# A second chunk transposed by DMA, the loads behind it rearranged, and the inverse 32-point units moved next to the forward ones

## The chip, the cores and the metric

One core of one Trainium2 chip. Times are device microseconds of one execution; the profile gives the span of that execution, some 1.9 us less. A ratio is the mean time of one kernel's fast runs over that of the kernel before in the same rounds on the same chip, so it is not quite the ratio of the medians. Kernels are compared only within the same rounds.

On one core a run counts as slow when it is over 1.5% above the fastest of the same kernel.

## The reference, cut to what matters

```python
# x: [1, 2048, 512] bf16; w_r, w_i: [2048, 257]; w_gate, w_up: [512, 1792]; w_down: [1792, 512]
xn  = layernorm(x)                              # rows of 512
A   = irfft2(rfft2(xn) * (w_r + 1j * w_i))      # 2048 x 512 transform, filter, inverse
B   = (gelu(xn @ w_gate) * (xn @ w_up)) @ w_down
out = x + A + B
```

## The kernel before: the parts that matter

TensorE does everything heavy. The gated unit (branch B) runs in four chunks of 512 rows, and the transform (branch A) is cut into small units that are slotted between its matmuls: "D" (along a row), "A" (64-point), "B" (32-point forward), "C" (32-point inverse), "E" and "F". Each unit's result is copied out of the matmul memory by ScalarE or VectorE (an eviction). Every step that follows another matmul group is a numbered hook; the plan puts calls at hooks. Each engine executes its own list in order.

The transposed, normalised rows `xnT` feed both branches; on the way to the D units VectorE adds and subtracts halves of them (the butterflies). Chunks 2 and 3 are transposed by DMA, chunk 1 (the second) by TensorE:

```python
if m < 2:
    at(t, (trans, m, (0, 1), (0, 1, 2, 3)))            # 8 TensorE transposes, copy by VectorE
    at(t + 1, (trans, m, (2, 3), (0, 1, 2, 3), "act")) # 8 more, copy by ScalarE
else:
    at(n + 1, (trans_dma, m))                          # one DMA transpose, issued by SyncE
```

A transform unit "A" of one quarter is stored to DRAM and reloaded in another layout; the first B reads all four quarters:

```python
def units_A(m):        # ... matmuls, eviction by ScalarE, then four stores:
    dma("act" if late_one and ri else "sp", scr1[...], tt[i]...)
def load_tv(m):        # two reloads; each waits until the quarter's stores have landed
    dma("sp", tv[...], scr1[...], r=[("scr1", 2 * m + g, ri) for g in range(2) for ri in range(2)], ...)
def unit_B(g):
    op("pe", ..., r=["be"] + TVK, ...)                 # TVK: every quarter's reload
```

The filter comes in eight slices, each of four loads on GpSimd's queue (`w_r`) and four on SyncE's (`w_i`); GpSimd copies its last column (number 256) apart. `load_late` makes a load wait until TensorE has come to the hook:

```python
def load_late(dst, src, keys, also=(), eng="pool"):
    op(eng, lambda e: e.dma_start(dst, src), ..., dma=True, after=[("pe", pr.cnt["pe"])])
# load_W(s): ... "sp" if k else "pool"
```

So SyncE's list carries the transposes, the stores and reloads of the quarters, and half of the filter. A load that stands ahead of a store in this list is issued ahead of it.

## Time and profile before

| | before |
|---|---|
| time, median (range) | 179.55 us (179.51 to 180.07) |
| span of the profiled run | 177.6 us |
| TensorE busy | 172.6 us, 97% |
| TensorE idle | 5.0 us, at the two ends |
| granted clock | 1.00 |

An engine at 97% busy over the whole span is read by its list: every microsecond of it is on the path, and whatever other engines do counts only where TensorE waits for it. The lines are in the prediction. SyncE's timeline (start, length, what): the stores and the reload of the third quarter, and the stores of the last one, whose reload at 64.58 us is in the prediction:

```profile
52.86 3.65 SPq L346 DMA_DIRECT2D scr<-early  x4
58.39 1.17 SPq L346 DMA_DIRECT2D tv<-scr  x2
59.60 1.94 SPq L346 DMA_DIRECT2D scr<-early  x3
```

### The profile page before, as it was taken

Reading aid. Unit: us, or ns where it says so; the run is one execution under the profiler, and the core shown is the slowest. Engines: PE = TensorE matmul, PEld = TensorE weight load, DVE = VectorE, ACT = ScalarE, POOL = GpSimd, SP = SyncE. Lnnn points to the kernel's source line nnn. Section 1 sums busy time; section 2 is a strip of 40 time slices with the busy share of each in tenths; the row PEclk is TensorE's granted clock in tenths of the full one; section 3 lists DMA queues with packets and bytes.
Section 4 is the critical chain, followed back from the end, with each engine's and each line's share of the span. In section 5 each row is a group of like instructions: output and inputs, shape, how many; then the busy total and the mean of one; then the engine's idle time right before and its main releaser. Section 6 shows DMA issues by size and latency. Waiting matters only on the chain.

```text
span 177.6 us, 3792 instructions
## 1 busy us (share of the span) xinstructions
PE 172.6 (97%) x1394; PEld 107.0 (60%) x1394; DVE 132.3 (74%) x329; ACT 93.5 (53%) x156; POOL 54.3 (31%) x107
## 2 busy tenths in 40 slices
PE   7999999999999999999999999999999999999992
PEld 2576564544566666566564655566766666656881
DVE  2768899986478967776785649797877777897552
ACT  3343557763677523546666665336678577632110
POOL 2210534025142056394850000011444635530000
PEclk9999999999999999999999999999999999999999
DMA  4999999799998579679771304591166646551104
GB/s 122 292 271 318 314 278 340 188 177 225 189 182 173 142 209 193 99 219 226 211 202 28 103 15 122 107 318 52 31 117 108 124 97 118 92 90 30 30 6 118
DMA packets 31059, 27.89 MB, mean 157 GB/s; under 512 B 7120, under 2 KB 27984, under 8 KB 30912
## 3 DMA queue, kind: packets, MB, share of 16 engines
q1 hardware_dynamic: 25936, 19.75, 45.4%
q0 software_dynamic: 4272, 7.24, 19.0%
q10 hardware_dynamic: 832, 0.66, 1.4%
q8 instruction: 11, 0.18, 0.5%
q14 instruction: 8, 0.07, 0.1%
HBM read 18.19 MB, written 6.29 MB: 138 GB/s over the span
## 4 chain that ended last, share of the span: by engine, by line
PE 92%; DMA 4%; SPq 2%; DVE 0%; issue 0%
PE ps L906 27%; PE ps L890 27%; PE ps L792 25%; DMA wu<-in_B_w_up_dram 4%; PE ps L620 2%; SPq L346 2%; PE ps L846 2%; PE ps L648 2%; PE ps L595 2%; PE ps L495 1%; PE ps L467 1%; PE ps L466 1%; PE ps L498 1%; PE ps L463 1%; PE ps L464 1%; PE ps L422 1%
## 5 line engine op out<-in xcount | busy, mean ns | idle before, releaser
L890 PE MATMUL ps<-xnT,wg 128*128 128x512 f16 (+2 forms) x244 | 58.0, 362 | 0.2 <-DMA wg<-in_B_w_gate_dram 0.2
L906 PE MATMUL ps<-xnT,wu 128*128 128x512 f16 (+1 forms) x240 | 57.9, 365 | 0.3 <-DMA wu<-in_B_w_up_dram 0.3
L912 DVE TENSOR_TENSOR hT<-ps,gl 128x512 bf16<-128x512 f32 (+1 forms) x60 | 38.9, 652 | 21.7 <-PE ps L906 15.7
L894 ACT ACTIVATE gl<-ps 128x512 bf16<-128x512 f32 (+1 forms) x60 | 34.2, 569 | 38.5 <-PE ps L890 37.3
L906 PEld LDWEIGHTS ps<-xnT,wu 128*128 128x128 bf16 x240 | 22.5, 98 | 20.5 <-issue 0.8
L890 PEld LDWEIGHTS ps<-xnT,wg 128*128 128x128 bf16 x244 | 22.7, 98 | 16.3 <-issue 1.0
L349 POOL DMA_DIRECT2D wring<-in_A_w_r_dram x32 | 18.7, 637 | 14.6 <-PE ps L792 5.4
L657 POOL COPY tv<-tv 1x128 bf16<-1x128 bf16 x16 | 5.4, 338 | 42.0 <-ACT tv L655 41.9
L792 PE MATMUL ps<-wd,hT 128*128 128x256 bf16 x112 | 14.4, 273 | 0.0
L872 POOL DMA_DIRECT2D x_sb<-tv x16 | 13.2, 865 | 3.4 <-DVE tv L865 2.4
L606 DVE TENSOR_TENSOR early<-early,wring 128x1024 bf16<-128x1024 f16 x16 | 10.3, 687 | 3.8 <-ACT early L601 3.8
L811 ACT ACTIVATE ps<-ps 128x256 f32<-128x256 f32 x16 | 5.9, 371 | 12.9 <-PE ps L792 12.8
L393 DVE BATCH_NORM_STATS2 st<-x_sb 128x6 f32<-128x512 bf16 x16 | 10.6, 682 | 2.2 <-DMA x_sb<-in_A_x_dram 2.2
L792 PEld LDWEIGHTS ps<-wd,hT 128*128 128x128 bf16 x112 | 10.7, 98 | 2.5
L401 POOL TENSOR_TENSOR rstd<-vpe,mhalf 128x4 f32<-128x4 f32 (+2 forms) x6 | 5.0, 836 | 23.1 <-DVE vpe L400 23.1
L471 ACT ACTIVATE early<-ps 128x512 f16<-128x512 f32 x16 | 9.5, 597 | 4.2 <-PE ps L467 4.2
L792 PE MATMUL ps<-arena,xnT 128*128 128x256 f16 x91 | 11.4, 273 | 0.0
L852 ACT ACTIVATE tv<-ps 128x512 bf16<-128x512 f32 x16 | 9.5, 595 | 3.6 <-PE ps L846 3.6
L655 ACT ACTIVATE tv<-ps 128x512 bf16<-128x512 f32 x16 | 9.5, 595 | 3.2 <-PE ps L648 3.2
L601 ACT ACTIVATE early<-ps 128x1024 f16<-128x1024 f32 x8 | 8.2, 1023 | 4.8 <-PE ps L595 4.8
L792 PEld LDWEIGHTS ps<-arena,xnT 128*128 128x128 f16 x91 | 8.5, 98 | 2.3 <-DVE tw L815 0.2
L675 DVE TENSOR_TENSOR x_sb<-ps,tw 128x256 bf16<-128x256 f32 x16 | 6.7, 421 | 2.9 <-PE ps L792 2.6
(119 smaller groups left out, 236.7 us busy)
## 6 DMA issues: line engine op xcount, KB each, us to landing
wring<-in_A_w_r_dram POOLq DMA_DIRECT2D x32, 64.2 KB, 4.3
wring<-in_A_w_i_dram SPq DMA_DIRECT2D x32, 64.2 KB, 4.5
tv<-scr SPq DMA_DIRECT2D x8, 256.0 KB, 4.3
scr<-early SPq DMA_DIRECT2D x8, 256.0 KB, 2.8
wring<-scr SPq DMA_DIRECT2D x4, 512.0 KB, 6.5
x_sb<-tv POOLq DMA_DIRECT2D x16, 128.0 KB, 2.7
scr<-early SPq DMA_DIRECT2D x15, 128.0 KB, 3.8
out_dram<-x_sb SPq DMA_DIRECT2D x28, 64.0 KB, 2.1
```

Of the source, the lines that this page charges most:

```text
L349: op(eng, lambda e: e.dma_start(dst, src), w=list(keys) + list(also), dma=True, after=[("pe", pr.cnt["pe"])])
L393: op("dve", lambda e: e.bn_stats(st[:, j, :], x_sb[:, j, :]), r=[("x", j, 0), ("x", j, 1)], w=[("st", j)])
L471: op("act", lambda e: e.activation(x4.rearrange("p (a c r) -> p a c r", a=2, r=4), bank(bk).rearrange("p (a r c) -> p a c r", a=2, r=4), A ...
L606: op("dve", lambda e, k=k: e.tensor_tensor(pp[i][k], xc[i], W[k][g % 4][:, :, :, 0:256], ALU.mult), r=[("xc", i)] + [key for c in range(2) ...
L655: op("act", lambda e: e.activation(z, bank(bk).rearrange("p (a c) -> p a c", a=4), ACT.Copy, scale=SC_E), r=[("ps", bk)], w=[zk] + (TVK if ...
L792: ins = e.matmul(o, st_(f), mv(f), start=(f == 0 and step in (0, 5)), stop=(f == 6), skip_group_check=True)
L852: op("act", lambda e: e.activation(o2, bank(bk), ACT.Copy), r=[("ps", bk)], w=[ok] + (TVK if j < 2 else []))
L872: op("pool", lambda e: e.dma_start(x_sb[:, j, :], ys, accum_op=ALU.add), r=[yk + (0,), yk + (1,), ("x", j, 0), ("x", j, 1)] + acc(j), w=ac ...
L890: ins = e.matmul(bank(bg)[:, c], wg_sb[:, dc, fc * P:(fc + 1) * P], xnT[:, j1:j1 + len(h), dc, :], start=(dc == 0), stop=(dc == 3), skip_g ...
L894: op("act", lambda e: e.activation(gl[k % 3][:, 0:n], bank(bg)[:, 0:n], ACT.Gelu_apprx_tanh), r=[("ps", bg)], w=[("gl", k % 3)])
L906: ins = e.matmul(bank(bu)[:, 0:n], wu_sb[:, dc, fc * P:(fc + 1) * P], xnT[:, j0:j0 + len(jjs), dc, :], start=(dc == 0), stop=(dc == 3))
L912: op("dve", lambda e: e.tensor_tensor(hT[b % 2][:, fc, h0:h0 + n], bank(bu)[:, 0:n], gl[k % 3][:, 0:n], ALU.mult), r=[("ps", bu), ("gl", k ...
```

## The change

The intent: take 16 transposes off TensorE (the second chunk goes by DMA too), give the DMA engines room for it (down weights behind the transpose in SyncE's queue, filter slices later), and save changes of TensorE's tile mode (C directly behind B everywhere, small unit 1 beside the first B, small unit 3 with full columns). The core of the diff, cut at `...`:

```diff
-                op("pe", lambda e: e.matmul(bank(bk)[0:32, 0:64], mtb[:, 7], ME, ...),
-                   r=["mm", ("mt", 7)], w=[("ps", bk)])
-                op("act", lambda e: e.activation(row[:], bank(bk)[0:32, 0:64], ...
+                op("pe", lambda e: e.matmul(bank(bk)[:, 0:64], mtb[:, 4:8]..., ME, ...),
+                   r=["mm"] + [("mt", i) for i in (4, 5, 6, 7)], w=[("ps", bk)])
+                op("act", lambda e: e.activation(row[:], bank(bk)[96:128, 0:64], ...
...
-            at(10 + 2 * i, (load_late, wd_sb[:, f0:f1, :], ...))
+            at(13 + i, (load_late, wd_sb[:, f0:f1, :], ..., (), "sp"))
...
-        for s, h0 in enumerate((30, 37, 49, 54, 61, 66, 70, 75)):
+        for s, h0 in enumerate((42, 46, 50, 54, 61, 66, 70, 75)):
             for i, t in enumerate(load_W(s)):
                 at(h0 + i // 2, t)
-            at(89 + s // 2 if s > 3 else (47, 48, 57, 58)[s], (keep_256, s))
+            at(89 + s // 2 if s > 3 else (52, 55, 57, 58)[s], (keep_256, s))
...
-            t = (16, 29, 35)[m - 1]
+            t = (20, 29, 35)[m - 1]
-            if m < 2:
-                at(t, (trans, m, (0, 1), (0, 1, 2, 3)))
-                at(t + 1, (trans, m, (2, 3), (0, 1, 2, 3), "act"))
-            else:
-                at(n + 1, (trans_dma, m))
+            at(n + 1, (trans_dma, m))
...
-            h = (11, 22, 35, 40)[m]
+            h = (11, 27, 35, 40)[m]
...
-                at(h + (g in (1, 5)), (unit_C, g - 1))
-            if g == 1:
-                at(h + 2, (mini, 1))
+                at(h + (g in ()), (unit_C, g - 1))
+            if g == 0:
+                at(h, (mini, 1))
```

## The prediction

> **What bounds the kernel now.** I began with the engine totals and the 40 slices. The program runs on one core with the clock granted in full, so no state enters.
>
> ```profile
> PE 172.6 (97%) x1394; PEld 107.0 (60%) x1394; DVE 132.3 (74%) x329; ACT 93.5 (53%) x156; POOL 54.3 (31%) x107
> PE   7999999999999999999999999999999999999992
> PEclk9999999999999999999999999999999999999999
> DMA  4999999799998579679771304591166646551104
> ```
>
> TensorE is busy in every slice but the first and the last. The idle 5.0 us (177.6 - 172.6) are the start, the first weights, and the last add with its store. The chain of waits says the same: 92% of it is TensorE, and the longest other piece is the first up weights before 11.5 us, which the change does not touch. So two things can move the end: TensorE work taken out, or new TensorE idle put in. VectorE, ScalarE and GpSimd savings count only through a wait of TensorE, and the waits of TensorE name none of them after 12 us.
>
> The chain in order of time then gives the price of each piece that the change touches (start, length, what):
>
> ```profile
> 24.38 0.45 PE ps L422 x8
> 25.69 0.45 PE ps L422 x8
> ...
> 74.19 0.34 PE ps L595 x8
> 74.53 0.87 PE ps L792 x7
> 75.40 0.56 PE ps L620 x16
> 75.96 0.97 PE ps L890 x4
> 76.93 0.13 PE ps L538 x4
> 77.06 0.87 PE ps L792 x7
> ...
> 83.70 0.34 PE ps L595 x8
> 84.04 0.44 PE ps L620 x16
> 84.48 0.97 PE ps L890 x4
> ...
> 110.78 0.13 PE ps L568
> 110.91 0.87 PE ps L792 x7
> ```
>
> L422 is the transpose of the second chunk, L595 the forward 32-point unit (B), L620 the inverse one (C), L538, L568 the small units of column 256, L792 a product step, L890 a gate. A product step is 0.76 to 0.77 and a gate 0.86 in undisturbed stretches; here they are 0.87 and 0.97 wherever the instruction before them used a smaller tile of the array.
>
> **What the Trainium skill says.** "TensorEngine Tiling (Array Packing)", section Key Properties: a change of tiling mode, not of tile, drains TensorE. The trace agrees and prices it: about 0.10 to 0.12 us at each entry and each exit (0.87 for 0.77, 0.97 for 0.86, C 0.56 alone for 0.44 behind B). "TensorE: Matmul & The Clock Gate", Part 4, gives about 275 ns for a 128x128 transpose inside a kernel, with a PSUM copy after it. Here one record is 219 ns, but they overlap: eight take 0.45 us of the chain, 56 ns each. I use 56. "DMA: Bandwidth & Descriptors", section Queues, rings and completion order: each DMA engine consumes a ring in order and goes round robin between queues. So a load moved from GpSimd's queue to SyncE's no longer shares the engines with what is ahead of it, it stands behind it. This trace cannot separate the two; from 20 to 34 us the two queues had 48.0% and 46.9% of the engines, which fits sharing. Same page, section DMA Transpose (X-bar): issued from SP or ACT only, two-byte types, destination SBUF; all are met here.
>
> **The change part by part.**
> 1. Second chunk by DMA. TensorE loses two groups of eight transposes: 2 x 0.45 = 0.90 us, all on the path. VectorE loses one copy of 0.69 us (busy 5.90 of 6.00 us from 24 to 30) and ScalarE one of 1.02; neither is on the path.
> 2. C behind B where they were apart, twice (at 75.4 and 95.1 us). Apart: 0.34 + 0.87 + 0.56 + 0.97 = 2.74. Together, with the same product step and gate: 0.34 + 0.44 + 0.97 + 0.76 = 2.51. Saved 0.23 each, 0.46.
> 3. Small unit 1 moved next to the first B, which has its tile mode: its 0.13 and the 0.10 of the step behind it become an estimated 0.04 (the 16 small matmuls of L555 behind a C cost 0.11). Saved 0.19.
> 4. Small unit 3 with all 128 columns as weights and a quarter of the result used: no mode change. 0.13 + 0.11 become an estimated 0.03 (64 columns at the pace of the transposes, 128 in 56 ns). Saved 0.21.
> 5. Moving the second chunk's transform units, down weights and filter slices removes no TensorE work.
>
> Sum: 0.90 + 0.46 + 0.19 + 0.21 = 1.76 us. Taken whole, 179.55 - 1.76 = 177.8.
>
> **What it may cost.** DMA has to do the work that TensorE drops, and stands in front of other transfers. The lines that matter (KB each, median us from issue to landing):
>
> ```profile
> xnT<-tw SPq DMA_TRANSPOSE x1, 6.0
> xnT<-cmx SPq DMA_TRANSPOSE x1, 7.9
> tv<-scr SPq DMA_DIRECT2D x2, 256.0 KB, 3.9
> 64.58 1.15 SPq L346 DMA_DIRECT2D tv<-scr  x2
> ```
>
> Rival A, the transform input. The normalised second chunk is ready at about 23.0 us (last of L412 in the VectorE timeline, 22.28 + 0.72), so the transpose can be issued then. The loads ahead of it in the queue are some 6.7 MB; the slices give 4.45 MB by 17.8 us and some 315 GB/s after that, and without the down weights on the other queue they end near 25 us. A transpose is 2048 packets of 256 B at a mean of 31 ns, so 4.0 us of all 16 engines: landing near 30. The butterflies moved from hook 18 to 22 stand near 30.6 us. That just fits, and the gate of this chunk comes only near 37. Behind it the down weights: the trace's packet records have 448 packets of 4 KB at some 230 ns on GpSimd's queue; in rows of 1 KB they are 1792 at a mean of 74 ns, so 8.3 us of the engines for 6.4. They are used only near 52 us, but the third transpose now queues behind them and may land near 42 to 43, where its butterflies stand at about 40.3 and its first transform unit at about 44.4; the butterflies take 2.2 us. So TensorE waits there for 0 to 1.3 us. For the rival: DMA is at 9 or 10 tenths until 30 us, and in the kernel before a butterfly already waits 1.1 us for a transpose. Against: filter slices no longer start at hook 30 (41.5 us), which frees 2.6 us of engines per slice (1.46 for the packets of 514 B, 1.17 for the other half).
>
> Rival B, a new wait at the first B. B reads the last quarter of the transform, reloaded from DRAM. In the kernel before this reload is issued at 64.58 and 65.15 us and lands 3.9 later, at about 69.0; the first B starts at 70.38, a margin of 1.3 us. In the changed order SyncE issues four slices of filter (0.60 us each, waiting for TensorE until 56.8 and 57.7 us) ahead of the quarter's store and two more ahead of its reload. In the old clock: filter 59.6 to 62.0, store 62.0 to 63.9 where it was 59.6 to 61.5, landing about 67, reload 67 to 68.2, landing about 72. That is 1.6 us after 70.38, and the filter traffic beside it (two extra slices, 5.2 us of engines in a stretch of 20 us that is 83% busy) can make it 3. TensorE would stand for 1 to 3 us, and the gain would be gone: 178.8 to 180.8. For: SyncE issues in order, and the hooks put the slice first. Against: these hooks look tuned (42, 46, 50, 54 and the four copies of column 256 each placed singly), so whoever set them has probably looked at this gap; and landing times scatter between 3.4 and 6.3 us, so my 1.6 is weakly founded.
>
> Rival C, filter slices too late for VectorE. The last two slices may land near 77 and 79 us; their products come near 80.5 and 85. I expect no wait, and a late one would first stop VectorE, which has about one gate pair (1.7 us) in hand through PSUM banks.
>
> Rival D, nothing of part 1 is gained since DMA transposes slow the weights: all gate and up weights are ahead of the transpose in the queue, so it cannot delay them. I give it little: 179.0.
>
> **Range and chances.** Floor without waits: 177.8. I take half a chance that rival A or B costs something visible, on average 1 us when it does, so the middle is 177.8 + 0.5 = 178.3. The low end, 177.5, is the floor with an error of 0.3 for the small estimates of parts 3 and 4 and for a vanished VectorE backlog. The high end, 180.1, is rival B at some 2.3 us. Faster by 2% needs 175.96, that is 3.6 us out of TensorE, twice what I can count: 0.02. Slower by 2% needs 183.1, a stall of over 5 us: 0.03. Within 2%: 0.95.
>
> **What would show it.** TensorE busy should fall from 172.6 to about 170.9, with no L422 group of 16 but only the first chunk's eight; C at 0.44 behind every B but the last; no 128*32 form. The waits of TensorE should show whether L595 waits for a reload of tv (rival B) and whether the transform units L463 wait for VectorE (rival A); the waits of VectorE, whether L446 waits for the transposes. The down weights should land near 37 to 39 us. The prediction is wrong if TensorE's busy time falls by clearly less than 1.7 us, if its idle time grows by more than 2.5 us, or if a wait for weights appears early.

## The result, and the profile after

The changed kernel takes 185.67 us (184.16 to 185.89, four runs) against 179.81 for the kernel before in the same rounds: ratio 1.0304, interval 1.0242 to 1.0367. It is slower.

Totals and slices of the page after, and then the waits of TensorE (in total, times, longest):

```profile
PE 172.8 (94%) x1378; PEld 107.0 (58%) x1378; DVE 131.7 (72%) x328; ACT 92.5 (50%) x155; POOL 51.2 (28%) x103
PE   7779999999999993699999999999999999999993
PEclk9999999999999999589999999999999999999999
```

```profile
PE ps L595 <- DMA tv<-scr: 4.2, 1, 4.2
PE ps L906 <- DMA wu<-in_B_w_up_dram: 1.2, 1, 1.2
```

The hole is in one place. TensorE reaches the first B (L595) and waits 4.2 us for a reload of `tv`; in the slices behind it the clock is down. TensorE's busy time seems unchanged at 172.8 us, though 16 instructions went: matmuls at a reduced clock are longer, so a busy total is no measure of work where the clock moves. SyncE's timeline after and the chain of waits show how the hole comes about:

```profile
53.18 3.50 SPq L346 DMA_DIRECT2D scr<-early  x4
59.70 1.15 SPq L346 DMA_DIRECT2D tv<-scr  x2
60.90 2.66 SPq L349 DMA_DIRECT2D wring<-in_A_w_i_dram  x4
63.61 1.94 SPq L346 DMA_DIRECT2D scr<-early  x3
65.59 1.26 SPq L349 DMA_DIRECT2D wring<-in_A_w_i_dram  x2
68.86 1.16 SPq L346 DMA_DIRECT2D tv<-scr  x2
```

```profile
64.93 3.81 DMA scr<-early
...
69.43 5.41 DMA tv<-scr
74.84 0.14 issue
74.98 0.62 PE ps L595 x6
75.59 0.04 PE ps L538 x2
75.63 1.82 PE ps L906 x4
77.45 1.49 PE ps L792 x7
78.94 1.28 PE ps L890 x4
...
117.31 0.03 PE ps L568
117.34 0.76 PE ps L792 x7
```

Four filter loads (2.66 us) stand ahead of the last quarter's stores, and two more between them and the reloads. The stores start at 63.61 us where they started at 59.60, the reloads at 68.86 where it was 64.58. Taken hop by hop, from the third quarter's stores to its reload, to the last stores, to their reload, to its landing, the chain takes 6.52, 3.91, 5.25 and 5.98 us where it took 5.53, 1.21, 4.98 and about 4.4. It slipped by 1.0 + 2.7 + 0.3 + about 1.6, some 5.5 us; the margin of about 1.3 us that the kernel before had takes its part, and 4.2 us of wait remain. The 2.7 us are the four loads in front; the rest lies between the issue of transfers and their landing. Behind the wait a group of four matmuls that took 0.97 us at this place before takes 1.82, a product step of 0.77 takes 1.49. The last two lines are the tile-mode part at work: small unit 3 costs 0.03 us where it was 0.13, and the step behind it is back at 0.76 from 0.87.

The clock comes from the windows (window, its length, busy times, granted clock, DMA share, GB/s):

```profile
70.00:74.50 4.50, 0.79 (x8) 0.47 (x5) 1.33 (x5) 0.60 (x1) 0.00 (x0) 0.82 1.00 216
74.50:78.00 3.50, 3.02 (x20) 1.56 (x21) 1.47 (x4) 1.02 (x1) 1.95 (x4) 0.50 0.67 136
78.00:82.00 4.00, 4.00 (x39) 2.07 (x38) 2.42 (x6) 1.11 (x2) 2.02 (x7) 0.79 0.24 74
```

The Trainium skill, "TensorE: Matmul & The Clock Gate", Part 1, says that an idle window of about 3.4 us sets TensorE back to half its clock, and that this window runs freely. The trace agrees on the half, 0.50 of the clock behind a wait of 4.2 us, and not on a gap of 3.4 us: in windows of 0.25 us the clock falls at 72.8 us, 2.0 us after TensorE stopped. It is back at 79.7 us, so from 74.98 us on TensorE works at half speed for 4.7 us.

I split the span in three: up to the landing of the first up weights (the part before it is the same in all kernels here, yet scatters between 11.4 and 13.8 us over the fast profiles), from there to the start of the first B, and from there to the end.

| us | weights landed | from there to B | of it the wait | rest | from B to the end |
|---|---|---|---|---|---|
| before | 11.41 | 58.90 | 0 | 58.90 | 107.3 |
| after | 12.75 | 62.23 | 4.18 | 58.05 | 109.0 |

After less before: 1.34 (scatter of the start) - 0.85 (transposes) + 4.18 (wait) + 1.7 (behind B) = 6.4 us, which is 184.0 - 177.6.

### The profile page after: what moved, and what is told of

Read it like the earlier page. It is cut to its first block, busy times and chain, and to the rows that moved or that the text cites. A ratio compares the mean times of both kernels' runs of the same rounds, so it can differ in the third digit from the quotient of the medians.

```text
span 184.0 us, 3753 instructions
## 1 busy us (share of the span) xinstructions
PE 172.8 (94%) x1378; PEld 107.0 (58%) x1378; DVE 131.7 (72%) x328; ACT 92.5 (50%) x155; POOL 51.2 (28%) x103
## 4 chain that ended last, share of the span: by engine, by line
PE 84%; DMA 9%; SPq 3%; ACT 2%; issue 0%; DVE 0%
PE ps L906 26%; PE ps L890 24%; PE ps L792 22%; DMA wu<-in_B_w_up_dram 4%; DMA tv<-scr 3%; SPq L346 3%; DMA scr<-early 2%; PE ps L648 2%; PE ps L846 2%; PE ps L620 2%; PE ps L595 2%; PE ps L495 1%; PE ps L466 1%; PE ps L498 1%; PE ps L467 1%; ACT early L601 1%
## 5 line engine op out<-in xcount | busy, mean ns | idle before, releaser
L906 PE MATMUL ps<-xnT,wu 128*128 128x512 f16 (+1 forms) x240 | 58.8, 369 | 1.2 <-DMA wu<-in_B_w_up_dram 1.2
L657 POOL COPY tv<-tv 1x128 bf16<-1x128 bf16 x16 | 5.4, 340 | 41.5 <-ACT tv L655 41.4
L792 PE MATMUL ps<-arena,xnT 128*128 128x256 f16 x91 | 11.4, 273 | 0.0
L675 DVE TENSOR_TENSOR x_sb<-ps,x_sb 128x256 bf16<-128x256 f32 x16 | 6.7, 421 | 3.2 <-PE ps L792 3.1
```

Of the source, the lines that this page charges most:

```text
L792: ins = e.matmul(o, st_(f), mv(f), start=(f == 0 and step in (0, 5)), stop=(f == 6), skip_group_check=True)
L906: ins = e.matmul(bank(bu)[:, 0:n], wu_sb[:, dc, fc * P:(fc + 1) * P], xnT[:, j0:j0 + len(jjs), dc, :], start=(dc == 0), stop=(dc == 3))
```

## The experiments

Theories. **Order**: SyncE issues its list in order, and the filter loads set at hooks 44 to 48 stand in front of the last quarter's stores and reloads. **Traffic**: what delays the stores and reloads is the filter's bytes on the DMA engines, wherever they were issued. **Chain**: the second chunk's transpose and what follows it make the whole transform late, and the slices are innocent. A fourth question is what the loss behind the wait is.

Seventeen kernels ran. The check of the result passed them all, number 12 too, although a part of its filter is left out.

### 1. The tile-mode part alone

The diff's lines on small unit 3, small unit 1 and `unit_C`, applied to the kernel before.

> The kernel before with only the tile-mode part: C behind B at the two places, small unit 1 beside the first B, small unit 3 with 128 columns. If each mode change costs what the chain showed, TensorE loses 0.46 + 0.19 + 0.21 = 0.86 us and the time is 178.9 (ratio 0.995), with the first B at the same moment as before (near 70.4 us, or shifted only by the wait for the first up weights). If the price of a mode change was an artefact of modelled ends, the time stays at 179.8 and TensorE's busy time falls by under 0.3 us.

Ratio 0.9946 (0.9899 to 0.9993). Weights to B 58.85 us, so nothing moved ahead of B; from B to the end 106.7 us, 0.6 less than before. Right in kind, and less than the 0.86 counted; see the experiments without waits.

### 2. The late slices alone

```diff
 # kernel before
-        for s, h0 in enumerate((30, 37, 49, 54, 61, 66, 70, 75)):
+        for s, h0 in enumerate((42, 46, 50, 54, 61, 66, 70, 75)):
-            at(... else (47, 48, 57, 58)[s], (keep_256, s))
+            at(... else (52, 55, 57, 58)[s], (keep_256, s))
```

> The kernel before with only the filter slices (and their column copies) late. Theory 1 (order on SyncE: the filter halves of slices 0 and 1 stand ahead of the last quarter's store and reload): the reload is issued 4 us later, the first B waits 3 to 4.5 us for it, the clock drops, and the time is 185.5 to 187. Theory 3 (the transposed second chunk with the down weights behind it delays the transform chain, slices are innocent): no wait at B, 179.5 to 180.3.

Ratio 1.0337 (1.0293 to 1.0380): this part alone reproduces the whole loss without the second chunk's DMA transpose. SyncE's timeline, and TensorE's waits:

```profile
60.20 2.65 SPq L349 DMA_DIRECT2D wring<-in_A_w_i_dram  x4
62.90 1.98 SPq L346 DMA_DIRECT2D scr<-early  x3
64.91 1.28 SPq L349 DMA_DIRECT2D wring<-in_A_w_i_dram  x2
68.34 1.87 SPq L346 DMA_DIRECT2D tv<-scr  x2
```

```profile
PE ps L595 <- DMA tv<-scr: 4.1, 1, 4.1
```

The same order and the same wait as in the changed kernel. So the late slices are enough to cause the loss; that the chain theory adds to it is not yet excluded. The traces bear on it: the third quarter's stores start 40.4 us after the first up weights in the changed kernel and 41.5 us after them before (53.18 - 12.75, 52.86 - 11.41), so up to there its transform is early and not late.

### 3. The changed kernel with the old slice hooks

```diff
 # changed kernel
-        for s, h0 in enumerate((42, 46, 50, 54, 61, 66, 70, 75)):   # and keep_256 back as well
+        for s, h0 in enumerate((30, 37, 49, 54, 61, 66, 70, 75)):
```

> The changed kernel with the filter slices and their column copies back at the old hooks. Theory 1: the wait at the first B goes (under 0.5 us), the clock stays at 1.00, and what is left is the 1.76 us of work taken out: 178.0 to 178.6 (ratio 0.990 to 0.993). Theory 3: B still waits 3 us or more, 183 to 186. A rival in between (transposes now behind the slices again, so that butterflies are late): a wait of 0.5 to 2 us at a transform unit, 178.5 to 180.

A miss for me. Three executions took 185.5 to 186.6 us and one 179.42; the three are slow. The profile is of a slow run and again has 4.3 us at the first B. SyncE's timeline of it:

```profile
53.81 2.58 SPq L349 DMA_DIRECT2D wring<-in_A_w_i_dram  x4
56.44 3.36 SPq L346 DMA_DIRECT2D scr<-early  x4
61.68 1.17 SPq L346 DMA_DIRECT2D tv<-scr  x2
62.89 1.96 SPq L346 DMA_DIRECT2D scr<-early  x3
68.21 1.15 SPq L346 DMA_DIRECT2D tv<-scr  x2
```

Here the filter loads of slice 1 are ahead of the third quarter's stores, which start at 56.44 (52.86 before), and the rest follows late. So there was a reason to move the slices: with three transposes and the second quarter's later stores, SyncE's list is behind at the old hooks. The move only changed which quarter is held up. That explanation rests on a slow run; experiment 8 tests it with fast ones.

### 4. Useless matmuls in the gap

```diff
 # changed kernel
+        at(59, (fill, 16))     # 16 matmuls of 128x512 into a free bank, ahead of the first B
```

> The changed kernel with 16 matmuls of no use (16 x 0.216 = 3.5 us) just before the first B, in the time in which TensorE stands. If the clock drop is caused by TensorE's idleness, the granted clock stays at 1.00 behind it and the time falls by 2 to 2.6 us to 183.0 to 183.8, with a wait of under 1 us left at B. If the loss behind the wait has another cause (late filter slices, ScalarE and VectorE behind), it stays at 185 to 186.

Ratio 1.0093 (1.0037 to 1.0150) against 1.0304 without the filling. The clock is 0.997 in the profile; TensorE still waits 1.3 us after 3.5 us of filling, so the reload was 4.7 us late. The matmuls behind B run at full pace (the chain of waits):

```profile
74.10 0.38 PE ps L595 x6
74.48 0.04 PE ps L538 x3
74.52 0.97 PE ps L906 x4
```

From B to the end it takes 106.8 us instead of 109.0. So 2.2 us of the loss were the clock, and came from standing idle. The ratios differ by more, 0.021 or 3.8 us; their intervals leave room for both.

### 5. SyncE's halves of slices 0 and 1 behind the reload

```diff
 # changed kernel
-                at(h0 + i // 2, t)
+                at(h0 + i // 2 if i < 4 or s > 1 else 49 + 2 * s + (i - 4) // 2, t)
```

> The changed kernel with only SyncE's halves of filter slices 0 and 1 (eight loads) moved behind the reload of the last quarter; GpSimd's halves stay. Theory 1 (order on SyncE): the store is issued at 59.5 to 60.5 us instead of 63.6, the reload near 64.5 instead of 68.9, TensorE waits at the first B under 0.5 us, the clock stays at 1.00, and the ratio to the kernel before is 0.988 to 0.993. Theory 2 (traffic of the filter slices on the DMA engines, wherever issued): the store and the reload still take 4 and 5.4 us to land, so B waits 1.5 us or more and the ratio stays above 1.01. Theory 3 (the transform chain is late from the transposes on): the store is issued no earlier than 62 us.

Ratio 1.0135 (1.0061 to 1.0209). The stores started at 61.85 us, later than I expected, but in a run whose first weights landed 2.2 us later than before. The wait at B fell to 0.7 us, but there is a new one:

```profile
PE ps L620 <- DMA cmx<-c_cm: 2.7, 1, 2.7
```

On GpSimd's list the copy of column 256 waits for the slice and holds up the inverse constants that C reads (GpSimd's timeline):

```profile
73.75 0.19 POOL L584 COPY w<-wring 128x4 bf16<-128x4 bf16 x1 [6.61 <-DMA wring<-in_A_w_i_dram]
...
75.33 0.62 POOL L349 DMA_DIRECT2D cmx<-c_cm  x1
```

The wait named was removed as expected and the ratio was not: an in-order list elsewhere took it over.

### 6. The same eight loads issued by GpSimd

```diff
 # changed kernel, load_W
-   "sp" if k else "pool"
+   "sp" if k and s > 1 else "pool"
```

> The changed kernel with the same eight loads at the same hooks, issued by GpSimd instead of SyncE: the same traffic at the same moments, SyncE free of it. Theory 1: as the run before it, store at about 60 us, no wait at B worth a microsecond, ratio 0.988 to 0.997. Theory 2: the wait at B stays at 1.5 us or more, ratio above 1.01.

Ratio 0.9990 (0.9928 to 1.0052). The stores start at 60.06 us, the wait at B is 1.5 us, the clock stays. Bytes and hooks are the same as in the changed kernel; the list differs, and with it the queue that carries the bytes (experiment 12 keeps the queue). So order made most of the wait, and a remainder near 1.5 us belongs to something else: the last store's landing took 5.31 us in the chain of waits (at most 4.2 before).

### 7. As 5, with the down weights back on GpSimd's queue

```diff
 # kernel of experiment 5
-            at(13 + i, (load_late, wd_sb[:, f0:f1, :], ..., (), "sp"))
+            at(10 + 2 * i, (load_late, wd_sb[:, f0:f1, :], ...))
```

> As the first of these runs, with the down weights back on GpSimd's queue at the old hooks. If they hinder the transposes by sharing the engines, the second chunk's transpose lands 2 us later than in the first run of this set (there near 31 us), its butterflies on VectorE wait, and the time is 0.3 to 1 us longer than there. If sharing is harmless, the times are equal within 0.3 us.

I had expected under 1 us; it is 187.84 to 192.78 us in all four runs, ratio of its fast ones 1.0453. The profile (of a slow run) has these waits of TensorE and of VectorE:

```profile
PE ps L463 <- DVE arena L450: 5.7, 1, 5.7
```

```profile
DVE cmx L446 <- DMA xnT<-cmx: 6.3, 1, 6.3
```

The second chunk's transpose took 14.7 us to land with the down weights on the other queue; in the changed kernel its three transposes took 5.5 to 9.0. This part of the change does what it was made for, and with the down weights as before the DMA transpose of this chunk does not fit. Queue and hooks moved together here, so the run does not separate sharing the engines from being issued earlier.

### 8. Old hooks, GpSimd issuing slices 0 and 1

Experiments 3 and 6 together.

> The changed kernel with the slices at the old hooks, and SyncE's halves of slices 0 and 1 on GpSimd. The earlier run with the old hooks still waited 4.3 us at B, with the store of the last quarter issued at 62.9 us. If SyncE's own line is the cause there too (loads and reloads of earlier quarters ahead of it), the store is issued by 60.5 us and the wait at B falls under 1 us: ratio 0.988 to 0.995. If the transposes and the later transform of the second chunk keep the chain late, the wait stays over 2 us.

Ratio 0.9978 (0.9922 to 1.0033). No wait at B; the stores start at 60.88 us with weights landed at 12.07. So in experiment 3 too it was SyncE's list. New is a wait of 1.0 us at a transform unit, as VectorE waits 2.5 us for a transpose: by the place of the slices, early filter traffic against the transposes; in experiment 14, with the slices later, both are gone.

### 9 to 11. Other places for the slices

`(GpSimd's, SyncE's first hook)` for slices 0 to 3, and the hooks of their column copies, in the changed kernel:

```diff
-                at(h0 + i // 2, t)
+  9:  ((36, 38), (51, 49), (53, 52), (54, 56))   copies (47, 62, 66, 70)   slice 0 in a gap, the rest behind
+ 10:  ((45, 46), (51, 49), (53, 52), (54, 56))   copies (60, 62, 66, 70)   slice 0 between store and reload
+ 11:  ((49, 49), (51, 51), (53, 53), (55, 55))   copies (60, 62, 66, 70)   all behind the reload
```

> The changed kernel with slice 0 loaded in the gap after the second quarter's reload (hooks 36 to 39), slices 1 to 3 behind the reload of the last quarter, and the column copies of slices 1 to 3 at hooks 62, 66, 70, so that they do not hold up the loads of the inverse constants on GpSimd's line, which cost 2.7 us in the run that moved only SyncE's halves. Theory 1 with the traffic term that the GpSimd-issued run showed: no wait at the first B over 0.5 us, none at a C, clock 1.00, ratio 0.988 to 0.993. If the landing of the store alone (4 to 5 us since the second chunk's chain runs later) keeps the reload late, B waits 1 to 2 us and the ratio is 0.996 to 1.002.

> The changed kernel with the eight SyncE loads only re-ordered around the last quarter: slice 0's between its store and its reload, slice 1's behind the reload; column copies at 60, 62, 66, 70. Order theory: the store is issued within 0.5 us of 59.6 plus the start's shift, the wait at B falls from 4.2 to 0.5 to 2 us (slice 0's traffic is still ahead of the reload in the ring), ratio 0.990 to 1.002. If order did not matter, the wait would stay at 4 us.

> The changed kernel with all four first slices, both halves, behind the reload of the last quarter: no filter traffic at all before it. Order and traffic theory together: no wait at B (under 0.5 us); but slice 0 lands only near 71 to 72, so VectorE's first product may wait 1 to 2 us; ratio 0.988 to 0.998. If B still waits over 1 us here, neither order nor filter traffic is the cause and the transform chain itself is late.

Experiment 10: ratio 1.0076 (1.0031 to 1.0120), wait at B 1.1 us, stores at 59.16. Experiment 11: 1.0160 (1.0102 to 1.0218), no wait at B at all. Experiment 9: three of four runs slow; its slow profile has no wait at B either. So with order and filter traffic both gone the wait is gone, and the chain theory falls as a cause of it. But all three wait at C for the inverse constants, 1.6 to 3.8 us: the slices, now packed into fewer hooks, stand in front of those constants. My expectations for 9 and 11 missed that.

### 12. SyncE's eight loads kept, their bytes taken away

```diff
 # changed kernel, load_W; the rest of these tiles is cleared by GpSimd; wrong result on purpose
-   W[...][p0:p0 + 32, :, :, 0:KW],                        v[c][:, :, hs, :]
+   W[...][p0:p0 + 32, :, :, 0:(2 if k and s < 2 else KW)], v[c][:, :, hs, 0:(2 if ... else KW)]
```

> The changed kernel with SyncE's halves of slices 0 and 1 cut to 2 of 257 columns, same eight loads at the same place in SyncE's line (wrong result on purpose; the rest of these tiles is cleared by GpSimd). It keeps the issue time and takes the traffic away. Order theory: the store is still issued near 63.6 us and the wait at B stays at 3 to 4 us, ratio 1.015 to 1.03. Traffic theory: the wait falls under 1.5 us.

The profile is of a run that counts as slow:

```profile
60.80 2.89 SPq L349 DMA_DIRECT2D wring<-in_A_w_i_dram  x4
63.74 1.94 SPq L346 DMA_DIRECT2D scr<-early  x3
65.72 1.27 SPq L349 DMA_DIRECT2D wring<-in_A_w_i_dram  x2
68.78 1.17 SPq L346 DMA_DIRECT2D tv<-scr  x2
```

```profile
PE ps L595 <- DMA tv<-scr: 3.2, 1, 3.2
```

With next to no bytes the stores start as late as in the changed kernel and 3.2 of the 4.2 us stay. What went is in one hop: from the third quarter's stores (at 54.00) to its reload it is 5.60 us and not 6.52. That hop takes 4.9 to 7.8 us in the other versions, so a gain of 0.9 us may be scatter. The two fast runs (clock 0.997 and 1.000) give a ratio of 1.0090, so the expected 1.015 to 1.03 missed: a wait of about 3 us let the clock drop in two executions of four, and my range had the drop in. With the gains counted below (0.87 and 0.5 us), 1.0090 still is about 3 us of waiting in all (1.6 + 1.4); in the profile 0.7 us of TensorE's waits lie at an earlier transform unit. Order is thus most of the wait; for the bytes of these eight loads at most about 1 us is left, and that is not shown.

### 13 and 14. Towards no wait at all

```diff
 # 13: kernel of 9
-        for i, h0 in enumerate((54, 57, 63, 68)):       # inverse constants
+        for i, h0 in enumerate((41, 43, 57, 59)):
 # 14: changed kernel, slices 0 and 1 by GpSimd
+  slices ((36, 38), (40, 42), (50, 52), (54, 56))   copies (47, 52, 62, 66)
```

> The run with slice 0 in the gap and slices 1 to 3 behind the reload, with the loads of the inverse constants also moved, from hooks 54, 57, 63, 68 to 41, 43, 57, 59, ahead of the compressed slices. In the earlier run the first B no longer waited, but the first C waited 3.8 us for these constants (issued at 70.7 us, 8.7 us to land behind ten filter loads). If that was all that was left, no TensorE wait over 0.5 us remains after 13 us, the clock stays at 1.00, and the 1.76 us of work taken out show in full: ratio 0.988 to 0.993. If the constants' traffic delays the last quarter's store again, B waits 0.5 to 1.5 us and the ratio is 0.994 to 1.000.

> The changed kernel with slices 0 and 1 issued by GpSimd at hooks 36 to 43: behind the last transpose, ahead of the last quarter's store and off SyncE's line; slices 2 and 3 behind the reload. With GpSimd issuing them at the old hooks, B did not wait, but VectorE waited 2.5 us for a transpose and TensorE 1.0 us at a transform unit. If both of those come from the slices' place, neither wait is left over 0.5 us: ratio 0.988 to 0.993. If slice 1's traffic slows the store of quarters three and four, B waits 0.5 to 1.5 us: 0.994 to 1.000.

Experiment 13: 1.0019 (0.9979 to 1.0060), with 1.3 us at B. I had put such a wait down to the constants' traffic; 16 and 17 below wait as long without it, so that is not shown. Experiment 14: 0.9954 (0.9923 to 0.9986). In its profile TensorE waits nowhere over 0.2 us after the first weights. ScalarE appears in its chain of waits, though, near the first C:

```profile
73.80 0.37 PE ps L595 x8
74.17 0.02 issue
74.19 1.02 ACT early L601
75.22 0.91 ACT early L625
76.13 0.29 ACT ps L811
```

Where C stands right behind B, their two evictions follow each other, and a product step waits for the copy behind them. TensorE's timeline has the price:

```profile
75.28 1.03 PE L890 MATMUL ps<-xnT,wg 128*128 128x512 f16 x4
76.46 0.94 PE L792 MATMUL ps<-arena,hT 128*128 128x256 f16 x7 [0.15 <-ACT ps L811]
```

The product step starts 1.18 us after the gate's group, where the pace is 0.87 (76.60 to 77.47 in experiment 16, which parts the pair). The wait listed is 0.15 us, with modelled ends; by the starts it costs 0.31 us.

### 15. The tile-mode part again

> The tile-mode part alone on the kernel before, again, beside the two others on one chip: 0.86 us counted, so a ratio of 0.995 (the first time 0.9946, interval 0.990 to 0.999). If the second chunk's DMA transpose is worth its 0.90 us, the better of the other two is 0.005 below this one; if the transpose gives nothing back even without waits, they are equal.

Ratio 0.9988 (0.9947 to 1.0029), so less than the first time, with intervals that overlap. On this chip experiment 14 is 0.003 below it; the expected 0.005 is not contradicted and not shown by these times. Its profile fell on a slow run and is not used for times; only a wait in it is counted in the last section.

### 16 and 17. The first C apart again, and 14 repeated

```diff
 # kernel of 14
-                at(h + (g in ()), (unit_C, g - 1))
+                at(h + (g in (1,)), (unit_C, g - 1))
```

> The version without waits (slices 0 and 1 by GpSimd in the middle) with only the first C put back one hook behind its B, as in the kernel before. In the version without waits the part behind the first B was 0.5 us shorter than before where 0.86 had been counted, and ScalarE stood in the chain there: two evictions of 1.02 us back to back ahead of a copy that a product step waits for. If that is what gave 0.35 us back, the chain has no ScalarE piece near the first C, the part behind the first B is 0.6 us shorter than before (0.86 less the 0.23 of this pair), and the ratio is 0.001 below its neighbour's. If the loss is elsewhere, the part is 0.3 us shorter than before and the ratio 0.001 above.

> The version without waits once more, beside the run above on one chip: first time 0.9954 (interval 0.9923 to 0.9986). Expected again 0.992 to 0.997, no wait of TensorE over 0.5 us after 13 us in the profile.

Experiment 16: 0.9941 (0.9897 to 0.9985), 179.44 us. Experiment 17: 1.0015 (0.9961 to 1.0069), outside the 0.992 to 0.997 that I expected of the same kernel. ScalarE is gone from 16's chain, and from B to the end it takes 106.7 us against 106.8 in its neighbour. Both wait 1.3 to 1.4 us at B in their profiles, where the same kernel did not wait in experiment 14: there is no margin left at B, and the landing of the last reload decides.

The pieces of the profiles of fast runs:

| us | from weights to B, less wait and filling | wait at B | from B to the end |
|---|---|---|---|
| before | 58.90 | 0 | 107.3 |
| 1 tile modes alone | 58.85 | 0 | 106.7 |
| after | 58.05 | 4.18 | 109.0 |
| 4 gap filled | 58.0 | 1.25 (and 3.46 of filling) | 106.8 |
| 6 by GpSimd | 58.03 | 1.47 | 106.8 |
| 14 by GpSimd, middle | 58.01 | 0 | 106.8 |
| 16 first C apart | 58.02 | 1.31 | 106.7 |

## Why the prediction was wrong

It said 178.3 us, within 177.5 to 180.1, and gave 0.03 to slower by over 2%. Measured: 185.67. Its own sign of being wrong is there: TensorE's idle time grew from 5.0 to 11.2 us, and it had allowed 2.5 more.

- **Part 1, 0.90 us for the transposes: right.** 58.90 us to B become 58.0 in every version: 0.87.
- **Parts 2 to 4, 0.86 us for the tile modes: right in kind, too large.** 0.5 us show from B to the end (107.3 to 106.8). Single terms were exact (small unit 3 at 0.03, small unit 1 at 0.04 us). In part 2 the first of the two pairs was priced on TensorE alone; ScalarE's two evictions in a row are then in the chain (14) and no longer when the pair is parted (16). They cost 0.31 us where 0.23 was to be saved, so that this pair is 0.1 us dearer together than apart, as the neighbours 16 and 17 differ. These 0.31 us are nearly all of the 0.36 us that are missing.
- **Rival A, the transform input: right.** The transposes fitted, and TensorE waited for no butterfly. Moving the down weights was undervalued: I counted that the loads ahead end earlier, and what it costs. Without it TensorE waits 5.7 us (experiment 7).
- **Rival B, a new wait at the first B: the mechanism as written, its size wrong. This is the step that failed.** I put the stores at 62.0 and the reload at 67.0 in the old clock, landing near 72, a wait of 1.6 us. Measured, less the 0.5 us by which this run is shifted (1.34 - 0.85): stores 63.1, reload 68.4, landing 74.3. The stores were 1.1 us later than I put them (0.8 as the third quarter's reload ahead of them was issued at 59.70 instead of 58.39, 0.3 as four loads took 2.66 us for 2.4), the reload's issue another 0.3, its landing another 0.9. The filter loads ahead of the stores, which I had, are 2.7 of the 5.5 us of slip; the rest is landings that I took at the length they had before, 4 us for the reload where it was 5.4. Whether the slices' traffic lengthened them is not shown: without the bytes of SyncE's eight loads the reload still takes as long (experiment 12). Small slips add up where each transfer waits for the landing of the one before it.
- **The clock: not in the sum at all.** I cited the page on the clock gate for transposes and took idle time as costing its own length. 4.2 us of standing cost another 2.2 us (experiment 4); by the same measure, the time from B to the end, it is 1.5 to 2.5 us in the profiles of 2, 3 and 12.
- **The chances: wrong.** "Hooks that look tuned" is no measurement; it halved the weight of a wait that the order of issue made plain. Experiment 2 shows that this part alone loses 3.4%.

The sum now: -0.87 - 0.5 + 4.2 + 2.2 = 5.0 us, 2.8% of 179.8, where the ratio says 3.0% (2.4 to 3.7).

Not settled: why the last reload lands up to 1.5 us after TensorE reaches B even with the filter moved (6, 13, 16, 17), and not in 14. The traces have the delay in different hops: from the third quarter's stores to its reload in 17 (7.81 us; 6.35 in 14, the same kernel), from the last stores to their reload in 6 (6.76; 4.61 in 14), from that reload to B in 13 (6.43). Of the 1.3 us of margin that the kernel before had, no version with the second chunk's DMA transpose keeps any for sure. The best version found, 16, is 0.6% faster than before by its interval (0.2 to 1.0%), which is weak for the best of several when one kernel had 0.9954 and 1.0015 (14 and 17), and 3.5% below the changed kernel (0.9941 over 1.0304); of the 1.37 us that its parts are worth in the profile, a wait takes some back in many executions.

## What to carry to other kernels

A queue that issues in order is a resource like an engine: before a load is moved, write down what stands behind it in that list and how much margin the next dependent store and reload have. A transfer chain of store, landing, reload, landing has no slack to average over, so each hop's delay adds. And when TensorE is the bound, price a wait of about 2.6 us or more as wait plus a reduced clock afterwards (eight of the nine such waits profiled here had it); useless matmuls in the gap are a quick test of how much of the loss is the clock.

## What the Trainium skill lacked or had wrong

- "TensorE: Matmul & The Clock Gate", Part 4: about 275 ns for a transpose in a kernel. That is near the 219 ns of one record here, but no price in a row: eight took 0.45 us of the chain, 56 ns each, at a clock of 1.00, and taking 16 out shortened the way to B by 0.87 us.
- The same page, Part 1, names an idle window of about 3.4 us. Here the clock fell 2.0, 2.8, 3.0 and 5.0 us after TensorE stopped (changed kernel, 3, 12, 2; in 2 after it had started again), and stayed at 0.50 for 3.4 or 6.8 us. Of nine profiled waits from 2.6 to 5.7 us all but one, of 2.7 us (experiment 5), were followed by half the clock, and none of 1.9 us or less after the first weights. Executions of one kernel differ by it: two of four in experiment 12 had the drop, with times from 181.6 to 185.2 us.
- "TensorEngine Tiling (Array Packing)", Key Properties, names the drain at a mode change but no price: 0.10 to 0.12 us at each entry and exit here. Padding a 32-column matmul to 128 columns took it from 0.13 us plus 0.11 at the next step to 0.03.
- "DMA: Bandwidth & Descriptors", Issuing engines are not separate DMA queues, says that issuing from several engines saves only the sequencer's time, usually small. Here the same eight loads moved from SyncE to GpSimd brought a wait of TensorE from 4.2 to 1.5 us: one load costs over 0.6 us of an in-order list (2.66 us for four), and a chain of transfers stood behind them.
- The same page, DMA Transpose (X-bar), has no time from issue to landing for a transpose from SBUF to SBUF. For 512 KB the trace has 5.5 to 9.0 us to landing in the changed kernel, and 14.7 with the down weights issued earlier on another queue; issuing it held SyncE for 3.5 to 5.5 us there.
